# A sparse attention and a gated mixture on one core: one list of works, played in time, sets every engine's order

## The chip, the cores and the metric

The kernel runs on one core of a Trainium2 chip. The metric is the time of one execution in device microseconds. Before the change it took 1155.85 us (median of 3 runs, 1151.24 to 1165.65). A core has five engines with a queue each: TensorE (PE), VectorE (DVE), ScalarE (ACT), GpSimd (POOL) and SyncE (SP), which here only issues DMAs. Matmuls write to PSUM, which has eight banks; all the rest lives in SBUF.

## What is computed

```python
scores = scale * q @ k.T                      # 8 batches x 8 heads, 576 x 576, head size 64
scores = where(scores >= max(scores) - tau, scores, -1e9)
attn = exp(scores - max(scores)); attn /= sum(attn) + 1e-9
x = (attn @ v)  # heads side by side: batch x 576 x 512
theta = x @ w_theta
y = w_tok_r @ (x * cos(theta)) + w_tok_i @ (x * sin(theta))      # over the 576 tokens
u = x + y
out = u + maximum(u @ w_ch, 0)
```

The weights come in as 64-bit floats; the two token matrices are stacked into one, so there are three to convert.

## The kernel before

**Tiles.** Two heads make a pair; there are 32 pairs, four to a batch. A pair's scores are cut into nine *half scores* of 128 x 576 (288 in all): one for the tails of both heads (the last 64 queries, `tail_h`, `tail_l`), and eight for 128 queries of one head each. Numbers are split into a high and a low part (`qh`, `kh`, `kl`, `xh`, `xl` ...), so that products of the parts come near fp32. Keys are moved by DMA (`spread_k`) so that both parts of a query can stand on 128 partitions.

**Attention, per half score.** Four matmuls into the one pair of score banks (`s_ps`, line 293), DVE empties them with the minimum of the negated scores (`sc`, 299) and adds the threshold (312), ACT takes the exponential (316), DVE masks it and sums the row (317), PE transposes it (343, 358), ACT copies the result out of PSUM (348 to 365). After half a pair PE multiplies by the values (`o_ps`, 378).

**Mixture, per batch.** In `moe`: `angle` multiplies x by w_theta (`m_ps`, 419); ACT evicts it divided by 2 pi (`th`, 457), DVE rounds it (`km`, 462) and subtracts (463). `sines` loads a table, takes four sines, loads the table of the exponential again (476 to 485). `flip` transposes (504), `token` multiplies by the token weights (521) and adds to x (524), `split_u` splits the sum (100, 104, 109), and the last product ends in line 569 and the store, 574. The mixture of one batch runs while the attention of the next does. Its weights are read back per product from DRAM by a load on POOL's queue (193), into three buffers.

**Weights.** `load_weight` turns a 64-bit float into two fp32 terms by passes of ACT and DVE; for two matrices PE adds the two in PSUM (160, 161), for the third DVE (151). Then ACT copies the high part and DVE subtracts it for the low part (100, 109).

**Order.** PE's order is written by hand: per half score the score three half scores ahead, then some mixture work up to an even share (`fill`), then this half score's transposes. On the other engines a scheduler orders the instructions by priorities (`ATTENTION`, `SINES`) and its own estimate of time, before the kernel runs; each engine then follows its fixed order.

Of the kernel before, what the change touches and what calls it, by code (L numbers as in the profile page):

```python
# [10 lines left out]
F32 = mybir.dt.float32  # L11
# [18 lines left out]
AHEAD = 3  # L30

ATTENTION, SINES = 20, 10000

LAG = 3

ORDER = "a0 a1 s01 a2 a3f0 s23 t0f1 t1f2 t2f3 t3"
# [3 lines left out]
def tile_attn_moe(  # L40
# [10 lines left out]
):  # L51
    nc = tc.nc
    B, NP, _, D, S = qT.shape
    P = 128
# [4 lines left out]
    NK = 9  # L59

# [3 lines left out]
    ps_s = ctx.enter_context(tc.tile_pool(name="ps_s", bufs=1, space=PSUM))  # L64
    ps_t = ctx.enter_context(tc.tile_pool(name="ps_t", bufs=6, space=PSUM))

    @contextmanager
    def at(offset, step=1):

        here = tc.cur_priority  # L70
        tc.cur_priority = max(0, here + offset)
        yield
        tc.cur_priority = here + step

    ident = const.tile([P, P], F32, name="ident")
    make_identity(nc, ident)

    small = const.tile([P, 4], F32, name="small")
    tau_sb = small[:, 0 : 1]
    nc.sync.dma_start(tau_sb, tau.broadcast_to([P, 1]))  # L80

    root = math.sqrt(D)
    gate = small[:, 1 : 2]
    span = small[:, 2 : 3]
# [3 lines left out]
    half_pi = small[:, 3 : 4]  # L88
    nc.vector.memset(half_pi, 0.5 * math.pi)
# [4 lines left out]

    def pool_copy(out, in_):
        nc.gpsimd.tensor_scalar(out=out, in0=in_, scalar1=1.0, scalar2=0.0, op0=ALU.mult, op1=ALU.add)

    def copy(eng, out, in_):
        if eng is nc.scalar:
            nc.scalar.copy(out=out, in_=in_)  # L100
        elif eng is nc.gpsimd:
            pool_copy(out, in_)
        else:
            eng.tensor_copy(out=out, in_=in_)

    def split(eng_hi, eng_lo, hi, lo, src):

        copy(eng_hi, hi, src)
        eng_lo.tensor_tensor(out=lo, in0=src, in1=hi.bitcast(F32), op=ALU.subtract)  # L109

    def temp(name, dt=F32):
        return pool.tile([P, S], dt, tag="t576", name=name, bufs=4)

    def after(ins, other, wait=False):

        kind = mybir.DependencyClass.Sync if wait else mybir.DependencyClass.NoSync
        info = mybir.DependencyInfo(kind, mybir.DependencyReason.DATA)
        tc.add_manual_dep(ins.ins, other.ins.name, info, reason="order")
        return ins

    turn = [0]

    def load_weight(src, n, on_pe=True):

        w = pool.tile([P, S], F32, tag="xh", name="w", bufs=4)[:, :n]
        if src.dtype == F32:
            nc.sync.dma_start(w, src)
            yield
            return [(slice(0, n), w)]
        turn[0] += 1  # L130
        tag, bufs = ("wm", 3) if turn[0] % 2 else ("z", 3)
        raw = pool.tile([P, S, 2], U32, tag=tag, name="wraw", bufs=bufs)[:, :n]
        nc.sync.dma_start(raw, src.bitcast(U32).rearrange("p (n t) -> p n t", t=2))
        low, high = raw[:, :, 0], raw[:, :, 1]
        bits = pool.tile([P, S], U32, tag="xh", name="bits", bufs=4)[:, :n]
        mag = pool.tile([P, S], U32, tag="xl", name="mag", bufs=4)[:, :n]
        magf, bitsf = mag.bitcast(F32), bits.bitcast(F32)
        yield
        nc.scalar.activation(out=magf, in_=high.bitcast(F32), func=AF.Abs)
        nc.vector.tensor_scalar(out=magf, in0=magf, scalar1=W_LEAST, scalar2=W_MOST, op0=ALU.max, op1=ALU.min)  # L140
        yield
        nc.vector.tensor_scalar(
            out=bits, in0=mag, scalar1=3, scalar2=0x3FFFFFFF, op0=ALU.logical_shift_left, op1=ALU.bitwise_and
        )
        nc.vector.scalar_tensor_tensor(
            out=bits, in0=high, scalar=0xC0000000, in1=bits, op0=ALU.bitwise_and, op1=ALU.bitwise_or
        )
        nc.vector.tensor_scalar(out=mag, in0=bits, scalar1=0xFF800000, scalar2=None, op0=ALU.bitwise_and)
        nc.vector.scalar_tensor_tensor(out=w, in0=low, scalar=2.0**-52, in1=magf, op0=ALU.mult, op1=ALU.mult)
        if not on_pe:  # L150
            nc.vector.tensor_tensor(out=w, in0=w, in1=bitsf, op=ALU.add)
            yield
            return [(slice(0, n), w)]
        yield

        n2 = n if n <= 512 else n // 2
        got = []
        for c in range(0, n, n2):
            ps = ps_t.tile([P, 512], F32, tag="t", name="w_ps")[:, :n2]
            nc.tensor.matmul(ps, ident, bitsf[:, c : c + n2], start=True, stop=False)  # L160
            nc.tensor.matmul(ps, ident, w[:, c : c + n2], start=False, stop=True)
            got.append((slice(c, c + n2), ps))
        return got

    def load_wtok(c):
        got = yield from load_weight(w_tok[c * P : (c + 1) * P, :], S)
        for r, w in got:
            split(nc.scalar, nc.vector, wt_h[:, c, r], wt_l[:, c, r], w)

    def load_wm(which, src, c):  # L170
        got = yield from load_weight(src[c * P : (c + 1) * P, :], DM, which == 0)
        hi, lo = (pool.tile([P, DM], F32R, tag="zh4" if x == "whi" else "zl4", name=x, bufs=4) for x in ("whi", "wlo"))
        for r, w in got:
            split(nc.scalar, nc.vector, hi[:, r], lo[:, r], w)
        for i, t in enumerate((hi, lo)):
            nc.sync.dma_start(
                wm_dram[which, :, :, i, c, :].rearrange("m p e -> p m e"),
                t.bitcast(F32).rearrange("p (m e) -> p m e", e=P),
            )

    def all_loads(todo):
        for fn, a in todo:
            yield from fn(*a)

    loads = [(load_wm, (0, w_theta, c)) for c in range(NM)]
    loads += [(load_wtok, (c,)) for c in range(NK)]
    streams = [all_loads(loads[i::2]) for i in range(2)]

    late = all_loads([(load_wm, (1, w_ch, c)) for c in range(NM)])

    def get_wm(which, m):
        t = pool.tile([P, 2, NM, P], F32R, tag="wm", name=f"wm{which}", bufs=3)
        nc.gpsimd.dma_start(t, wm_dram[which, m].bitcast(F32R))  # L193
        return t

    tails = []
    for x in ("h", "l"):
        t = const.tile([P, P], F32R, name="tail_" + x)
        nc.gpsimd.memset(t.bitcast(F32), 0.0)
        tails.append(t)  # L200

    v5_t = []
    for i in range(3):
        v5 = const.tile([P, 2, D], F32, name=f"v5{i}")
        nc.gpsimd.memset(v5, 0.0)
        v5_t.append(v5)

    xT = {}
    pairs = {}

    def move(out, in_):
        nc.sync.dma_start(out.bitcast(F32), in_.bitcast(F32))  # L212

    def load_raw(n, src, name):
        raw = temp(name)
        nc.sync.dma_start(raw, src[n // NP, n % NP].rearrange("j d s -> (j d) s"))
        return raw

    def prepare_q(n):
# [492 lines left out]
```

## Time and profile before

| | |
|---|---|
| median of 3 runs | 1155.85 us |
| profiled execution | 1148.71 us |
| its span | 1146.9 us |
| busy: PE, DVE, ACT, POOL | 1033.3, 821.2, 682.8, 271.2 us |
| mean granted clock of PE | 0.987 |
| DMA: packets, data | 95116, 143.07 MB |

A matmul is pipelined: its busy time (about 0.3 us) is longer than the distance to the next (0.13 us), so a busy PE need not be at its pace. A wait is put down to what came last. Lines are those of the kernel before.

### The profile page before, as it was taken

The numbers are of one execution on the slowest core, as the hardware profiler recorded it, in microseconds if no ns is written. First come the engines' busy times: TensorE is split into PE (matmuls) and PEld (weight loads), VectorE is DVE, ScalarE is ACT, GpSimd is POOL, SyncE is SP. The second block draws the span as 40 slices with busy tenths as digits, with TensorE's granted clock in tenths as the row PEclk, the third lists the DMA queues.
The fourth block names the chain that finished last, engine by engine and source line by source line (L and its number), as shares of the span: only waits on it lengthen the run. The fifth ranks groups of instructions, "written<-read, shape, count | busy, mean of one in ns | idle before, by whom it ended". The sixth has DMA issues, their size and how long they took to land.

```text
span 1146.9 us, 21522 instructions
## 1 busy us (share of the span) xinstructions
PE 1033.3 (90%) x7608; PEld 907.0 (79%) x7608; DVE 821.2 (72%) x2105; ACT 682.8 (60%) x1324; POOL 271.2 (24%) x233
## 2 busy tenths in 40 slices
PE   2988899799989998999989998999899999899998
PEld 1666687688878877898778987898878988788898
DVE  4899776976768676776767767777767768686452
ACT  3666768655576556854567546764577555764350
POOL 0002014221143122420234213311234212430210
PEclk9989999989999999999999999999999999999999
DMA  7764544465543274444633364533544355430411
GB/s 240 205 187 116 134 119 113 125 178 143 145 119 97 68 201 118 114 103 113 177 106 96 93 180 126 133 94 90 164 118 118 96 138 159 117 86 12 140 51 60
DMA packets 95116, 143.07 MB, mean 125 GB/s; under 512 B 35488, under 2 KB 43680, under 8 KB 95008
## 3 DMA queue, kind: packets, MB, share of 16 engines
q1 hardware_dynamic: 85792, 108.12, 35.5%
q0 software_dynamic: 9216, 33.56, 10.3%
q8 instruction: 61, 1.00, 0.4%
q14 instruction: 47, 0.39, 0.1%
HBM read 71.37 MB, written 13.63 MB: 74 GB/s over the span
## 4 chain that ended last, share of the span: by engine, by line
PE 49%; DVE 15%; ACT 15%; DMA 9%; SPq 6%; issue 5%; ACTq 0%; DVEq 0%
PE y_ps L521 13%; PE s_ps L293 9%; PE o_ps L378 8%; PE m_ps L419 8%; SPq L212 6%; PE t_ps L343 5%; DVE s_sb L317 4%; DMA qraw<-in_qT_dram 3%; DVE sc L299 3%; ACT s_sb L316 3%; DMA kraw<-in_kT_dram 2%; ACT z L480 2%; DMA qq<-qraw 2%; DVE xl L109 2%; ACT L476 2%
## 5 line engine op out<-in xcount | busy, mean ns | idle before, releaser
L317 DVE SCALAR_TENSOR_TENSOR s_sb<-sc,nm,s_sb 128x576 f32<-128x576 f32 x288 | 264.2, 917 | 79.4 <-ACT s_sb L316 74.4
L316 ACT ACTIVATE s_sb<-sc,nm 128x576 f32<-128x576 f32 x288 | 224.2, 779 | 153.7 <-DVE sc L299 153.3
L299 DVE TENSOR_SCALAR_CACHE_REDUCE sc<-s_ps 128x576 f32<-128x576 f32 x288 | 216.6, 752 | 113.9 <-PE s_ps L293 111.4
L293 PE MATMUL s_ps<-k,qq 128*128 128x288 f32 x1024 | 195.1, 313 | 56.4 <-DVE sc L299 48.5
L293 PEld LDWEIGHTS s_ps<-k,qq 128*128 128x128 f32 x1024 | 151.9, 193 | 73.9 <-DVE sc L299 63.6
L348 ACT COPY a<-t_ps 128x512 f32<-128x512 f32 x256 | 147.3, 578 | 68.0 <-PE t_ps L343 67.4
L378 PE MATMUL o_ps<-a,v 128*64 128x256 f32 (+1 forms) x1280 | 175.9, 422 | 1.1 <-ACT a L350 1.0
L343 PE MATMUL t_ps<-ident,s_sb 128*128 128x128 f32 x1152 | 174.7, 275 | 0.0
L521 PE MATMUL y_ps<-wt_h,zh 128*128 128x288 f32 x576 | 165.3, 305 | 4.8 <-ACT zh L506 4.8
L521 PE MATMUL y_ps<-wt_l,zh 128*128 128x288 f32 x576 | 163.2, 301 | 0.0
L343 PEld LDWEIGHTS t_ps<-ident,s_sb 128*128 128x128 f32 x1152 | 142.6, 141 | 2.1 <-issue 0.8
L378 PEld LDWEIGHTS o_ps<-a,v 128*64 128x64 f32 x1280 | 90.4, 141 | 65.4 <-issue 12.9
L193 POOL DMA_DIRECT2D wm<-wm_dram x64 | 36.2, 565 | 349.6 <-PE m_ps L419 318.3
L521 PEld LDWEIGHTS y_ps<-wt_h,zh 128*128 128x128 f32 x576 | 108.9, 189 | 5.5 <-ACT zh L506 5.5
L521 PEld LDWEIGHTS y_ps<-wt_l,zh 128*128 128x128 f32 x576 | 109.0, 189 | 0.0
L521 PE MATMUL y_ps<-wt_h,zl 128*128 128x288 f32 x576 | 102.8, 304 | 0.0
L419 PE MATMUL m_ps<-uh,wm 128*128 128x288 f32 x512 | 84.5, 300 | 11.5 <-ACT uh L100 11.5
L228 POOL TENSOR_TENSOR qraw<-qraw,qh 128x576 fp32r<-128x576 f32 x31 | 44.3, 1429 | 212.7 <-ACT qh L226 206.8
L419 PE MATMUL m_ps<-xh,wm 128*128 128x288 f32 x512 | 90.0, 305 | 3.0 <-ACT a L348 2.5
L492 POOL TENSOR_TENSOR z<-z,xT 128x576 f32<-128x576 f32 x56 | 82.8, 1508 | 29.4 <-ACT z L480 29.4
L521 PEld LDWEIGHTS y_ps<-wt_h,zl 128*128 128x128 f32 x576 | 83.5, 189 | 0.0
L419 PEld LDWEIGHTS m_ps<-uh,wm 128*128 128x128 f32 x512 | 72.0, 188 | 13.8 <-ACT uh L100 13.3
(90 smaller groups left out, 1541.5 us busy)
## 6 DMA issues: line engine op xcount, KB each, us to landing
wm<-wm_dram POOLq DMA_DIRECT2D x64, 512.0 KB, 4.6
qraw<-in_qT_dram SPq DMA_DIRECT2D x32, 288.0 KB, 3.0
kraw<-in_kT_dram SPq DMA_DIRECT2D x32, 288.0 KB, 3.2
k<-kh SPq DMA_DIRECT2D x64, 144.0 KB, 2.5
k<-kl SPq DMA_DIRECT2D x64, 144.0 KB, 2.7
out_dram<-xT SPq DMA_DIRECT2D x32, 288.0 KB, 4.5
qq<-qh SPq DMA_DIRECT2D x64, 128.0 KB, 2.4
qq<-qraw SPq DMA_DIRECT2D x64, 128.0 KB, 2.4
```

The costliest lines, as they stand in the source:

```text
L212: nc.sync.dma_start(out.bitcast(F32), in_.bitcast(F32))
L228: eng.tensor_tensor(out=lo, in0=raw, in1=hi.bitcast(F32), op=ALU.subtract)
L293: nc.tensor.matmul(ps[:, h, :HS], st, kk[:, h * HS : (h + 1) * HS], start=(x == 0), stop=(x == len(parts) - 1))
L299: nc.vector.tensor_scalar(out=sc.rearrange("p (a b) -> p a b", a=2), in0=ps[:, :, :HS], scalar1=-1.0, scalar2=None, op0=ALU.mult, op1=ALU.min,
L316: nc.scalar.activation(out=e, in_=u.ps[j], func=AF.Exp, bias=nm[:, j : j + 1], scale=-1.0)
L317: nc.vector.scalar_tensor_tensor(out=e, in0=u.ps[j], scalar=nm[:, 2 + j : 3 + j], in1=e, op0=ALU.is_le, op1=ALU.mult, accum_out=u.pr.rows[ ...
L343: nc.tensor.transpose(out=tp[:, c * P : (c + 1) * P], in_=u.sf[:, k0 + c * P : k0 + (c + 1) * P], identity=ident)
L348: nc.scalar.copy(out=t.a[:, :, j, q0 : q0 + P], in_=tp.rearrange("p (c q) -> p c q", c=4))
L378: nc.tensor.matmul(o[64 * j : 64 * j + 64, :w], st, mv, start=(c == 0), stop=(c == 4))
L419: nc.tensor.matmul(tiles[h][:, :HS], wm[:, a, c, :], parts[c][bb][:, hs], start=(count[h] == 0), stop=(count[h] == 11))
L492: lo_eng.tensor_tensor(out=zi, in0=zi, in1=x, op=ALU.mult)
L521: nc.tensor.matmul(ps[:, :HS], z, w, start=(n == 0), stop=(n == len(work) - 1))
```

## The change

The file is written anew around a list. Each piece of work is entered with its engine, a fixed duration, the works that it needs, the buffers that it takes and a rank; `Plan.run` plays the list, always taking the work that can start first, by rank where several can, and emits the instructions in that order, for all five engines. Attention's half score h has the rank 3.2 h; its passes have offsets from it; the mixture's works are spread over the ranks of the next batch.

```diff
+    def run(self):
+            for e in engines:
+                for w in wait[e]:
+                    at = max(free[e], w.ready)
+                    for p, n in w.pots:
+                        at = max(at, p.soonest(n))
...
+                    best = (first, min((x for x in starts if x[0] <= first + 1e-6), key=lambda x: x[1].rank)[1])
...
+            free[w.eng] = at + w.busy
+            w.end = at + w.busy + w.lag + HOP
+            w.fn()
...
-        for r, w in got:
-            split(nc.scalar, nc.vector, wt_h[:, c, r], wt_l[:, c, r], w)
+                for k, x in enumerate(terms()):
+                    nc.tensor.matmul(bank.tile, turns if turn else ident, x[:, r], start=(k == 0), stop=False)
+                nc.tensor.matmul(bank.tile, minus, hi_of()[:, r], start=False, stop=True)
+            def low(r=r, bank=bank):
+                nc.scalar.copy(out=lo_of()[:, r], in_=bank.tile)
...
-                nc.scalar.activation(out=th[:, hs], in_=ps[:, :HS], func=AF.Copy, scale=1.0 / TURN)
-            km = temp("km")
-            nc.vector.tensor_scalar(out=km, in0=th, scalar1=MAGIC, scalar2=-MAGIC, op0=ALU.add, op1=ALU.add)
-            nc.vector.tensor_tensor(out=th, in0=th, in1=km, op=ALU.subtract)
+                    nc.vector.tensor_scalar(
+                        out=th.tile[:, hs], in0=bank.tile[:, :HS], scalar1=MAGIC, scalar2=-MAGIC, op0=ALU.add, op1=ALU.add
+                    )
+                def rest():
+                    less(nc.vector, th.tile[:, hs], bank.tile[:, :HS], th.tile[:, hs])
...
-        nc.gpsimd.dma_start(t, wm_dram[which, m].bitcast(F32R))
+            nc.sync.dma_start(h.tile.bitcast(F32), wm_dram[which, m])
...
-            for r in (slice(0, 64), slice(64, P)):
-                if j == 0:
-                    move(t[r], src)
+                    move(pr.kd[j].tile[dst, :, to], pr.kk.tile[src, :, fr])
...
-            split(nc.scalar if c == NM - 1 else nc.vector, nc.vector if c == NM - 1 else nc.gpsimd, hi, lo, xT[b * NP + c])
+            us[m] = halves_of(m, "u", False, m < 3 and not last, adds, here() - STEP)
```

**Low parts of weights by PE.** PE sums the two terms of a weight and, with a negated identity, the high part; what is left in PSUM is the low part, which ACT copies out. This now holds for all three matrices. **Angles as turns.** The first matrix is scaled by 1 / 2 pi while it is converted, so the product in PSUM counts turns; DVE rounds each half of it straight from PSUM and subtracts. **Moves.** The high and low parts of queries and keys lie in one tile (`qhl`, `khl`), so that tails and keys move in half as many DMAs; a pair's values come in one load. **Other.** The mixture's weights are read back on SP's queue. The last high part of u is made on DVE, not ACT, and the first channel product of a batch takes the fourth tile last. The list's durations are constants, such as 0.76, 0.13 and 0.82 us for the three DVE passes of a half score, 0.67 for DVE's subtraction of a whole tile, and 0.131 for a matmul.

The order on SP at the start, before: `qraw`, `kraw` are the first pair's loads, `wraw` weights, `qh` and `qraw` the parts of its queries; the moves of its keys (`k_0_0`) follow.

```order
L80 DMA small<-in_tau_dram 128x1
L216 DMA qraw_93<-in_qT_dram 128x576
L133 DMA wraw<-in_w_theta_dram 128x1024 x4
L133 DMA wraw<-in_w_tok_dram 128x1152
L216 DMA kraw_109<-in_kT_dram 128x576
L216 DMA qraw_209<-in_qT_dram 128x576
L212 DMA tail_h<-qh_95 64x64 x2
L212 DMA tail_l<-qraw_93 64x64 x2
L212 DMA qq_0_103<-qh_95 64x512
```

And of the change, the same place; `kd` are moved keys, `64x1152` a half with both parts.

```order
L385 DMA qraw<-in_qT_dram 128x576
L385 DMA kraw<-in_kT_dram 128x576
L466 DMA v<-in_vp_dram 128x640
L245 DMA wraw<-in_w_theta_dram 128x1024
L385 DMA qraw<-in_qT_dram 128x576
L245 DMA wraw<-in_w_theta_dram 128x1024
L466 DMA v<-in_vp_dram 128x640
L217 DMA qq<-qhl 64x512
L217 DMA kd<-khl 64x1152
L217 DMA tails<-qhl 64x2x64 x2
L217 DMA kd<-khl 64x2x512
L217 DMA qq<-qhl 64x512
```

The load of the keys moved ahead of the weights, two loads of weights moved behind the first moves, and the moves of keys stand among those of queries and tails.

The order on DVE in the middle, where a batch's x is split and its first angle is done, before (`sc` empties scores, `s_sb` masks):

```order
L109 TENSOR_TENSOR xl<-xT_4327,xh 128x576
L109 TENSOR_TENSOR xl<-xT_4730,xh 128x576
L317 SCALAR_TENSOR_TENSOR s_sb,rows_4749<-sc,nm,s_sb 128x576
L312 TENSOR_SCALAR nm<-nm,small 128x1
L299 TENSOR_SCALAR sc,nm<-s_ps 128x576
```

And of the change, the split and, a little later, an angle's halves:

```order
L214 TENSOR_TENSOR xl<-xT,xh 128x576
L511 TENSOR_SCALAR sc,nm<-s_ps 128x576
L214 TENSOR_TENSOR xl<-xT,xh 128x576
L522 TENSOR_SCALAR nm<-nm,small 128x1
L537 SCALAR_TENSOR_TENSOR s_sb,rows<-sc,nm,s_sb 128x576
L511 TENSOR_SCALAR sc,nm<-s_ps 128x576
L537 SCALAR_TENSOR_TENSOR s_sb,rows<-sc,nm,s_sb 128x576
L522 TENSOR_SCALAR nm<-nm,small 128x1
L537 SCALAR_TENSOR_TENSOR s_sb,rows<-sc,nm,s_sb 128x576
L511 TENSOR_SCALAR sc,nm<-s_ps 128x576
L817 TENSOR_SCALAR th<-m_ps 128x288
```

Between the two subtractions for x an emptying now stands, and the roundings of angles (817) read PSUM by halves between the passes of attention.

The order on SP in the middle of the change (before, the loads `wm` stood in POOL's queue):

```order
L998 DMA out_dram<-xT 128x576
L217 DMA kd<-khl 64x1152
L358 DMA wm_3357<-wm_dram 128x1024
L217 DMA kd<-khl 64x2x512
L217 DMA kd<-khl 64x1152
L385 DMA qraw<-in_qT_dram 128x576
L217 DMA kd<-khl 64x2x64
L217 DMA kd<-khl 64x2x512
```

A load of the mixture's weights, which waits for PE to free one of three buffers, moved in between two moves of a pair's keys.

## Rows read from the trace of the kernel before

**Rows 1.** timeline of TensorE: start us, busy us, engine, line, operation, count
```profile
144.55 2.38 PE L378 MATMUL o_ps<-a,v 128*64 128x256 f32 x20
...
603.71 0.60 PE L343 MATMUL t_ps<-ident,s_sb 128*128 128x128 f32 x4
604.14 0.60 PE L504 MATMUL z_ps<-ident,z 128*128 128x128 f32 x4
605.07 2.91 PE L378 MATMUL o_ps<-a,v 128*64 128x320 f32 x20
```

**Rows 2.** stretches: length, busy us (x instructions) by engine, PE clock, DMA share, GB/s
```profile
0.00:146.90 146.90, 106.37 (x603) 78.34 (x603) 115.80 (x309) 89.87 (x175) 19.46 (x25) 0.98 0.61 173
146.90:289.00 142.10, 126.02 (x931) 110.85 (x929) 109.15 (x275) 86.42 (x167) 35.00 (x28) 0.96 0.53 141
289.00:421.30 132.30, 124.03 (x943) 110.17 (x941) 95.54 (x247) 81.95 (x160) 35.45 (x29) 0.99 0.46 122
...
818.50:949.90 131.40, 124.02 (x941) 110.19 (x942) 95.49 (x247) 82.01 (x160) 35.41 (x29) 0.99 0.46 122
949.90:1075.20 125.30, 117.93 (x906) 105.47 (x906) 85.94 (x226) 74.59 (x146) 28.93 (x25) 1.00 0.35 92
1075.20:1146.90 71.70, 64.09 (x474) 62.00 (x473) 32.50 (x60) 21.62 (x37) 10.79 (x11) 1.00 0.23 75
sum 1146.90, PE 1033.30 PEld 907.05 DVE 821.19 ACT 682.85 POOL 271.20; mean PE 114.81 PEld 100.78 DVE 91.24 ACT 75.87 POOL 30.13
```

**Rows 3.** chain that ended last, in order of time: start us, us, what
```profile
1119.59 9.17 PE y_ps L521 x69
```

**Rows 4.** TensorE's waits, 289.0 to 949.9 us: total, times, longest
```profile
PE s_ps L293 <- DVE sc L299: 21.8, 24, 2.2
PE z_ps L504 <- ACT th L457: 10.2, 5, 2.0
PE m_ps L419 <- ACT uh L100: 7.6, 5, 1.5
```

**Rows 5.** timeline around the end of a block of sines, [idle before <- releaser]
```profile
581.64 1.28 ACT L485 ACT_TABLE_LOAD   x1
582.94 0.41 ACT L457 ACTIVATE th<-m_ps 128x288 f32<-128x288 f32 x1
583.49 0.91 PE L504 MATMUL z_ps<-ident,z 128*128 128x128 f32 x4 [2.04 <-ACT th L457]
```

**Rows 6.** ten microseconds around it, columns as in rows 2
```profile
580.00:590.00 10.00, 7.82 (x51) 5.60 (x51) 6.16 (x11) 7.79 (x16) 5.64 (x4) 0.83 0.30 92
```

**Rows 7.** timeline of TensorE at the start
```profile
22.71 0.58 PE L293 MATMUL s_ps<-k,qq 128*128 128x288 f32 x1 [6.23 <-DMA k<-kh]
```

**Rows 8.** instructions by form: shapes, count | busy us, mean ns | idle, releaser
```profile
L109 DVE TENSOR_TENSOR wt_l<-w_ps,wt_h 128x288 fp32r<-128x288 f32 x18 | 7.8, 449 | 0.2
L109 DVE TENSOR_TENSOR wlo<-w,whi 128x512 fp32r<-128x512 f32 x4 | 3.2, 789 | 0.7 <-ACT whi L100 0.7
L457 ACT ACTIVATE th<-m_ps 128x288 f32<-128x288 f32 x64 | 26.5, 417 | 13.0 <-PE m_ps L419 12.6
L462 DVE TENSOR_SCALAR km<-th 128x576 f32<-128x576 f32 x32 | 18.4, 573 | 28.1 <-ACT th L457 21.0 <-DMA qq<-qh 7.1
L463 DVE TENSOR_TENSOR th<-th,km 128x576 f32<-128x576 f32 x32 | 31.9, 996 | 0.3
L524 DVE TENSOR_TENSOR xT<-y_ps,xT 128x288 f32<-128x288 f32 x64 | 28.8, 450 | 9.1 <-PE y_ps L521 9.1
L109 DVE TENSOR_TENSOR ul<-xT,uh 128x576 fp32r<-128x576 f32 x8 | 6.0, 754 | 0.7 <-ACT uh L100 0.7
L109 DVE TENSOR_TENSOR xl<-xT,xh 128x576 fp32r<-128x576 f32 x16 | 23.6, 1509 | 0.5 <-ACT xh L100 0.5
```

**Rows 9.** timeline of VectorE at the halves of x
```profile
557.86 3.19 DVE L109 TENSOR_TENSOR xl<-xT,xh 128x576 fp32r<-128x576 f32 x2
```

**Rows 10.** longest wait of all engines: us in total, times, longest
```profile
POOL wm L193 <- PE m_ps L419: 318.3, 47, 18.3
```

More of the change, by code (lines that the diff above doesn't have):

```diff
@@ new lines, with __init__ @@
+class Work:
+    def __init__(self, eng, busy, fn, need, rank, lag, takes):
+        self.eng, self.busy, self.fn, self.rank, self.lag, self.takes = eng, busy, fn, rank, lag, takes
+        self.need = [w for w in need if w is not None]
+        self.frees, self.users, self.end, self.ready = [], [], None, 0.0
+        self.left = len(self.need)
+        self.pots = [(p, sum(h.pot is p for h in takes)) for p in {h.pot: 0 for h in takes}]
+        for w in self.need:
+            w.users.append(self)
@@ new lines, in tile_attn_moe, with pot, hold, get @@
+    pots = {}
+    def pot(name, n):
+        pots[name] = Pot(name, n)
+    for name, n in (
[3 rows of a table added]
+    ):
+        pot(name, n)
+    def hold(name):
+        return Hold(pots[name])
+    def get(h, shape, dt=F32, name=None, tag=None):
+        tag = tag or h.pot.name
+        p = psum if tag in ("pair", "bank") else pool
+        return p.tile(shape, dt, tag=f"{tag}{h.slot}", name=name or tag, bufs=1)
+    PACE, TURN_PACE = 0.131, 0.109
+    def on_pe(n, fn, need, rank, takes=(), pace=PACE, lag=0.165, extra=0.0):
+        return plan.add("PE", n * pace + extra, fn, need, rank, lag + 0.027, takes)
@@ L121, in tile_attn_moe @@
[L121 to L163, printed above, removed]
@@ L196, in tile_attn_moe, with less @@
[L196 to L209, printed above, removed]
+    def less(eng, out, a, b):
+        eng.tensor_tensor(out=out, in0=a, in1=b, op=ALU.subtract)
     def move(out, in_):
         nc.sync.dma_start(out.bitcast(F32), in_.bitcast(F32))
[L214 to L217, printed above, removed]
@@ new lines, in tile_attn_moe, with load_wm, load @@
+    last_wm = [None]
+    def load_wm(which, m, rank):
+        h = hold("wm")
+        def load():
+            h.tile = get(h, [P, 2, NM, P], F32R, f"wm{which}")
+            nc.sync.dma_start(h.tile.bitcast(F32), wm_dram[which, m])
+        h.load = on_sp(load, wm_ready[which] + [last_wm[0]], rank, (h,), 4.2)
+        last_wm[0] = h.load
+        return h
+    halves = [(n, i, j) for n in range(B * NP) for i in (4, 0, 1, 2, 3) for j in range(2 if i < 4 else 1)]
+    pairs = {}
+    score_pe = {}
@@ L667 @@
+    plan.run()
 def kernel(**inputs):
```

1122 lines of the change are left out of this document (699 added, 423 removed), and 3 rows, old and new, of the table pots.

## The prediction

> **What bounds the kernel now.** I cut the span where the last value product of each batch ends (144.55 + 2.38 = 146.9 us for the first [rows 1], and so on) and read the busy times of the stretches [rows 2]. Over the span TensorE (PE) is busy 1033 of 1147 us, VectorE (DVE) 821; but a busy PE is not a PE at its pace, and the stretches differ. There are four kinds: the first batch of attention with the conversion of the weights (146.9 us), the second with the rest of it (142.1), then five alike, 660.9 us from 289.0 to 949.9, 132.2 each (attention of one batch with the mixture of the batch before), a last batch of attention (125.3), and a tail of 71.7 in which only the last mixture is left.
>
> What would PE need for one of the five? Its paces stand in dense rows: 69 token products in 9.17 us, 0.133 each [rows 3]; four transposes from 603.71 to 604.14, 0.108 each; a value product of 2.91 or 2.38 us [rows 1]. One batch holds 152 score, 192 channel and 216 token matmuls (560 x 0.133 = 74.5 us), 220 transposes (23.8) and four value products of either size (21.2): 119.5 us. The period of 132.2 is 12.7 above it. PE's three largest waits over the five periods are 21.8, 10.2 and 7.6 us [rows 4], 7.9 per period; the other 4.8 are small waits, a lower clock, and pauses that hide in the modelled ends of matmuls. So the middle is bound by PE, with a tenth of it holes, and the reader should see that what PE waits for is late for reasons of order. At 583.49 it waits 2.04 us for a PSUM bank whose angles ScalarE (ACT) reads only at 582.94, behind the table load that ends a block of sines [rows 5]; in the ten microseconds around it the granted clock is 0.83, between 2.4 and 1.2 GHz [rows 6]. The scores wait for a DVE that is late with emptying their banks.
>
> The first stretch is bound elsewhere: DVE is busy 115.8 of 146.9 us, PE 106.4 [rows 2]. The first whole scores start at 22.71 us, after 6.23 us of waiting for moved keys [rows 7].
>
> **The change part by part.** *The start.* In SP's new order the first keys are loaded third, and the moves that the first whole scores need stand second to seventh behind the loads, high and low part in one transfer; before, they stood behind weights, tails, the queries' moves and a load of values. Keys can then be split near 8 us, moved by 12 and landed some 2.5 us later: scores at about 15 instead of 22.71. I take 7 us off; the bounds are 0 (weights hold DVE and ACT instead) and 8.
>
> *Low parts of the weights.* In the first stretch DVE loses 18 subtractions of 0.449 us and 4 of up to 0.789 [rows 8], 11 us. PE gains 18 products of 288 columns and 4 of 512 (0.133, and 512/288 x 0.133 = 0.236): 3.3 us, hidden, since PE idles 40 there. ACT gains 22 copies of about 0.45 us (its nearest row is the eviction of 288 columns, 0.417), 10 us on an engine busy 90 of 147 [rows 2]; covered, and worth those 10 if it weren't. DVE is the bound, so I take 10 off, and 3 more because the list spreads thirteen conversions over 36 half scores where the order before has them within 22, so that DVE runs dry less. Stretch 1: 146.9 - 7 - 10 - 3 = 127. In stretch 2 DVE loses an addition and a subtraction, 0.789 each at most, for four pieces of the third weight matrix (6 us), and PE takes on about 5; PE was busy 126.0 of the 142.1 us [rows 2]. I take off the 6, and 6 of the 16 idle for the new order: 130.
>
> *Angles.* ACT loses 64 evictions of 0.417 us (26.5 us, 3.3 per batch). DVE loses 0.573 + 0.996 per angle and gains four passes over half a tile from PSUM. No row has these; the nearest is the addition of half a tile from PSUM, 0.450 [rows 8]. From below half of the rounding from SBUF bounds a pass (0.29), from above a subtraction of a whole tile (0.754). With 0.45, 1.80 stands against 1.57, 0.9 us per batch more; DVE idles 37 us per period and hides it, or 0.9 are lost. What it buys is that no bank of angles waits for a block of sines: PE's 2.0 us per period go, and with them 1.2 of the 1.7 us (0.17 x 10) that the clock costs there.
>
> *The order.* The wait for the last high part of u (7.6 us in five periods, 1.5 each) goes, since that copy leaves ACT and the first channel product takes the fourth tile last. Of the 4.4 us per period for which scores wait for DVE I take off 2.9: emptying has a low rank number, so that it is next when its scores are done, but a pass under way is never broken off. Another 0.8 are taken for the small waits. Per period: 132.2 - 2.0 - 1.2 - 1.5 - 2.9 - 0.8 = 123.8.
>
> *Contention, which the list does not know.* Its durations are fixed. The same subtraction of a whole tile takes DVE 0.754 us for the low part of u and 1.509 for that of x [rows 8]: at 557.86 two of the latter take 3.19 us [rows 9] while GpSimd (POOL) makes its own two. In the new order of DVE these two still stand close together. By the rows 1.5 us of the score waits stay for it, as above. The Trainium skill ("SBUF — State Buffer", Who interferes with whom) says that GpSimd and a DVE pass that contend for their shared port pair do not share it, the second one is fully blocked; the trace agrees (1.509 against 0.754), and by that rule the list's 0.67 us for x is too short in every period.
>
> *The last two stretches.* In the eighth some 5 us of the same go: 120. In the tail PE has 60.0 us of work behind the last value product where it had 61.6, by the same paces, and idles 7.6 [rows 2]; I take 1.6 and 1 off: 69.
>
> Sum: 127 + 130 + 5 x 123.8 + 120 + 69 = 1065 us of span, against 1146.9. The profiled execution's own time was 1148.7, 1.8 above its span, and the median shown, 1155.85, is 1.006 of that. So (1065 + 1.8) x 1.006 = **1073 us**.
>
> **The rivals.** *Slip eats the middle.* Every engine now follows a fixed order, so a pass of 1.5 us where the list has 0.67, or a late transfer, holds all that stands behind it. For it: the rows of xl. Against it: DVE and ACT were in an order fixed beforehand, too, and one that knew less. The middle then stays at 132.2, and the last two stretches where they were: 127 + 130 + 661 + 125 + 71.7 = 1115, 1124 us in time.
>
> *PE nearly full.* Holes and clock loss gone, the period is PE's own 119.5 us: 127 + 126 + 5 x 119.5 + 116 + 67 = 1033, 1041 us. Against it: 4.8 us per period stand in no large wait.
>
> *Little moves*: the change doesn't do what it says. DVE still bounds the first two stretches, at 140 each, and the middle gains 2 us per period: 140 + 140 + 651 + 124 + 71 = 1126, 1135 us, and up to the old time.
>
> *Slower: the mixture's weights block SP.* Their 64 loads move from POOL's queue to SP's. On POOL they waited 318.3 us for PE to give up a buffer, in 47 waits of 6.8 us on average [rows 10], and nothing on the path stood behind them. On SP one now stands between two moves of a next pair's keys. If the list thinks a buffer free when it is not, the keys behind it are late, and the scores with them: 6.8 us for each of 32 pairs are 218 us, 1292 in time. It decides for slower from 3.3 us per pair on (106 us, from 1073 to 1179, 2% above the median). Against it: the list has played PE's release itself, and keys have about two half scores (132.2 / 36 = 3.7 us each) in hand.
>
> **How the numbers follow.** Forecast, periods of 121 to 127 us: 0.62, which is 1058 to 1090. PE nearly full: 0.10. Slip: 0.15. Little moves: 0.08. Slower: 0.05. The range goes from 1035, just under the second case, to 1125, which takes in the slip; the last two stay out. The forecast's own range is 1050 to 1100. Faster by over 2%, about what a measurement of this kernel can tell from no change, is below 1132.7: the first three cases and a little of the fourth, 0.88; within 2% 0.07; slower 0.05.
>
> **What would show it.** In the profile after: first whole scores near 15 us and the first batch's end near 127; periods of 122 to 126 between the same points; no wait of PE for an angle's eviction, and no ten microseconds in the middle with a clock below 0.9; scores waiting for DVE about 1.5 us per period; xl still twice as long as ul on DVE. The forecast is wrong if periods stay above 129, which a wait of SP for PE among a pair's keys, or of ACT for a late transfer, would explain, or if they fall to 120, for then the unnamed 4.8 us were waits after all.

## The result and the profile after

The changed kernel takes **1083.61 us** (median of 4 runs, 1080.86 to 1087.21) where the kernel before, measured beside it, takes 1155.66: a ratio of 0.937, with a 95% interval of 0.930 to 0.944. It is faster by 6.3%, and 10.6 us above the forecast of 1073, inside the forecast's own range of 1050 to 1100. Of one kernel below, one execution of four ran at a granted clock of 0.75 and took 1322.29 us; the figure given for it is that of the other three.

The profiled execution has a span of 1078.8 us. Cut at the same points as before, where the last value product of each batch ends, it looks like this (columns: stretch and its length, busy time and count on PE, PE's weight loads, DVE, ACT and POOL, granted clock, DMA share, GB/s). The rows that answer to them are [rows 2].

```profile
core 0: us, PE busy (x) PEld busy (x) DVE busy (x) ACT busy (x) POOL busy (x), PEclk, DMA share, GB/s
0.00:126.20 126.20, 101.37 (x629) 76.57 (x629) 103.67 (x288) 92.46 (x184) 16.40 (x18) 1.00 0.75 204
126.20:258.20 132.00, 128.96 (x954) 112.02 (x952) 103.79 (x276) 86.35 (x164) 31.74 (x21) 1.00 0.56 150
258.20:383.90 125.70, 121.42 (x943) 109.33 (x941) 94.15 (x257) 80.03 (x151) 30.91 (x21) 1.00 0.50 130
383.90:511.20 127.30, 123.38 (x943) 110.90 (x942) 93.76 (x257) 80.05 (x151) 31.12 (x21) 0.99 0.49 128
...
889.00:1011.30 122.30, 119.08 (x914) 106.77 (x912) 87.07 (x240) 73.04 (x139) 25.16 (x17) 0.99 0.37 99
1011.30:1078.80 67.50, 62.17 (x460) 60.31 (x460) 35.88 (x69) 17.82 (x28) 3.04 (x2) 1.00 0.23 75
```

The other three periods are 125.0, 127.7 and 125.1 us, so five of them take 630.8 where they took 660.9.

| stretch | before | forecast | after |
|---|---|---|---|
| first | 146.9 | 127 | 126.2 |
| second | 142.1 | 130 | 132.0 |
| five periods, each | 132.2 | 123.8 | 126.2 |
| eighth | 125.3 | 120 | 122.3 |
| tail | 71.7 | 69 | 67.5 |
| span | 1146.9 | 1065 | 1078.8 |

Of the 13.8 us that the span is above the forecast, 11.8 lie in the five periods. There the groups of PE's waits, from 258.2 to 889 us, are now two (engine, tile and line, what ended the wait: us in total, times, longest). They answer to [rows 4]:

```profile
PE s_ps L497 <- DVE sc L511: 10.9, 14, 1.6
PE m_ps L775 <- ACT a L583: 9.0, 5, 1.8
```

The two old waits by ACT, for `th` and for `uh`, are gone, and the scores wait half as long. The second line is new. The timeline shows its place (start, duration, engine, line, operation, count; in brackets the idle time before it and what ended that), once in every period at the end of a block of sines; it answers to [rows 5]:

```profile
406.91 1.28 ACT L852 ACT_TABLE_LOAD   x1
410.13 0.67 ACT L856 ACTIVATE z<-th 128x576 f32<-128x576 f32 x1
410.83 0.82 DVE L817 TENSOR_SCALAR th<-m_ps 128x288 f32<-128x288 f32 x2 [0.49 <-ACT z L856]
412.11 1.07 ACT L583 COPY a<-t_ps 128x512 f32<-128x512 f32 x2
412.75 1.33 PE L775 MATMUL m_ps<-xh,wm 128*128 128x288 f32 x4 [1.80 <-ACT a L583]
```

DVE could round the next angle only when the last sine had read the old one, at 410.80: both stand in buffers of the kind `raw`, of which there are three. Until then the angle's two halves sat in two of the six shared PSUM banks, transposes waited in others for ACT, and PE found none for its next product. The clock falls behind it in the second and the fourth period, though the wait is as long in the others (1.7 to 1.8 us in all five); here is a stretch of ten microseconds, to set beside [rows 6]:

```profile
410.00:420.00 10.00, 8.05 (x51) 6.66 (x52) 6.76 (x21) 8.25 (x16) 6.17 (x5) 0.83 0.33 82
```

At the start PE's first products come at 13.23 us and the first whole scores at 17.71, against 22.71 in [rows 7], with no wait of their own: PE was busy with a weight's low part until then.

```profile
17.07 0.80 PE L302 MATMUL w_ps<-whi,minus 128*128 128x512 f32 x1
17.71 0.70 PE L497 MATMUL s_ps<-kd,qq 128*128 128x288 f32 x4
```

### The profile page after: what moved, and what is told of

It reads as the page before. It is cut to its first block, busy times and chain, and to the rows that moved or that the text cites. A ratio compares the mean times of both kernels' runs of the same rounds, so it can differ in the third digit from the quotient of the medians.

```text
span 1078.8 us, 21076 instructions
## 1 busy us (share of the span) xinstructions
PE 1022.4 (95%) x7650; PEld 905.0 (84%) x7650; DVE 800.1 (74%) x2152; ACT 669.9 (62%) x1269; POOL 231.1 (21%) x162
## 4 chain that ended last, share of the span: by engine, by line
PE 76%; DVE 8%; ACT 7%; DMA 5%; SPq 2%; issue 2%; POOL 0%; ACTq 0%; POOLq 0%; DVEq 0%
PE y_ps L933 22%; PE o_ps L650 13%; PE s_ps L497 12%; PE m_ps L775 12%; PE t_ps L572 9%; PE z_ps L885 3%; DMA qraw<-in_qT_dram 2%; DVE sc L511 2%; PE w_ps L301 2%; DMA kd<-khl 2%; SPq L217 2%; DVE xl L214 1%; PE t_ps L607 1%; DVE s_sb L537 1%; PE rb_ps L685 1%
## 5 line engine op out<-in xcount | busy, mean ns | idle before, releaser
L537 DVE SCALAR_TENSOR_TENSOR s_sb<-sc,nm,s_sb 128x576 f32<-128x576 f32 x288 | 247.1, 863 | 97.8 <-ACT s_sb L529 95.6
L497 PE MATMUL s_ps<-kd,qq 128*128 128x288 f32 x1024 | 186.1, 303 | 22.9 <-DVE sc L511 22.3
L497 PEld LDWEIGHTS s_ps<-kd,qq 128*128 128x128 f32 x1024 | 147.7, 188 | 35.8 <-DVE sc L511 32.1
L650 PE MATMUL o_ps<-a,v 128*64 128x256 f32 (+1 forms) x1280 | 170.2, 412 | 0.0
L933 PE MATMUL y_ps<-wt_l,zh 128*128 128x288 f32 x576 | 168.0, 308 | 0.0
L214 POOL TENSOR_TENSOR qhl<-qraw,qhl 128x576 fp32r<-128x576 f32 x31 | 46.4, 1497 | 460.6 <-ACT qhl L397 380.4
L650 PEld LDWEIGHTS o_ps<-a,v 128*64 128x64 f32 x1280 | 87.8, 137 | 61.2 <-issue 10.6
L933 PE MATMUL y_ps<-wt_h,zl 128*128 128x288 f32 x576 | 114.0, 306 | 0.0
L868 POOL TENSOR_TENSOR z<-z,xT 128x576 f32<-128x576 f32 x56 | 78.2, 1432 | 83.4 <-ACT z L855 83.4
L775 PE MATMUL m_ps<-uh,wm 128*128 128x288 f32 x512 | 92.2, 302 | 0.3 <-DVE uh L211 0.3
L775 PEld LDWEIGHTS m_ps<-xh,wm 128*128 128x128 f32 x512 | 76.0, 193 | 17.1 <-ACT a L583 11.8
```

What stands on the lines that cost most here:

```text
L214: eng.tensor_tensor(out=out, in0=a, in1=b, op=ALU.subtract)
L497: nc.tensor.matmul(ps.tile[:, half, :HS], st, kk[:, half * HS : (half + 1) * HS], start=(x == 0), stop=(x == len(terms) - 1),)
L537: nc.vector.scalar_tensor_tensor(out=e, in0=sc.tile, scalar=nm.tile[:, 1:2], in1=e, op0=ALU.is_le, op1=ALU.mult, accum_out=pr.rows.tile[:, ...
L650: nc.tensor.matmul(bank.tile[64 * j : 64 * j + 64, :w], st, mv, start=(c == 0), stop=(c == 4))
L775: nc.tensor.matmul(banks[h].tile[:, :HS], wm.tile[:, a, c, :], x[:, h * HS : (h + 1) * HS], start=(key == 0), stop=(key == 11),)
L868: eng.tensor_tensor(out=zi, in0=zi, in1=xs[m].x.tile, op=ALU.mult)
```

## The experiments

Four questions were put: what the new wait costs, what the two engines' meeting on x costs, which part of the change carries the gain, and whether the list needs its durations. One thing must be known to read them: under the list an edit changes the whole order, not the edited place alone, because every work is placed anew. Differences of a few microseconds between such kernels therefore hold more than the edit, and the four executions of one kernel already spread by 2 to 12 us (6.4 in the changed one).

| kernel | us | ratio to before, 95% |
|---|---|---|
| changed | 1083.61 | 0.937 [0.930, 0.944] |
| four `raw` buffers | 1071.09 | 0.929 [0.923, 0.934] |
| x split without POOL | 1068.87 | 0.926 [0.922, 0.931] |
| both of these | 1065.18 | 0.923 [0.919, 0.928] |
| angles by ACT, under the list | 1085.13 | 0.940 [0.935, 0.945] |
| weights converted earlier | 1085.47 | 0.941 [0.937, 0.945] |
| the same, low parts by DVE | 1099.34 | 0.953 [0.948, 0.957] |
| mixture's weights on POOL's queue | 1113.10 | 0.965 [0.961, 0.969] |
| flat durations | 1177.67 | 1.022 [1.016, 1.028] |
| before, angles by DVE | 1118.06 | 0.970 [0.965, 0.975] |
| before, mixture's weights on SP | 1137.16 | 0.986 [0.981, 0.991] |
| before, both | 1117.99 | 0.970 [0.965, 0.974] |

**A fourth buffer for angles.**

```diff
-("raw", 3)
+("raw", 4)
```

> The kernel of the change with a fourth buffer for raw loads, angles and the broadcast of row sums (raw 3 to 4), nothing else edited; the list is played again with it. In the trace of the change TensorE waits 1.80 us in each period for a PSUM bank at the end of the first block of sines (412.75, 540.05). Theory A: the bank is held since VectorE cannot evict the next angle before ScalarE has read the old one in its last sine (the rounding at 410.83 waits 0.49 us for that sine), that is, for want of a buffer. Then the wait and the fall of the clock after it go, about 1.8 to 2.5 us per period, and the time falls by 10 to 17 us, to about 1070. Theory B: the bank is held by copies of transposed scores that queue behind the block on ScalarE. Then the wait stays and the time is within 4 us of the change's.

Measured: 1071.09 us, 12.5 below the changed kernel (the profiled spans differ by 10.9), as theory A has it. The line of `m_ps` is gone from PE's waits, and the one that is left is this (from the first sines of the second batch to those of the seventh):

```profile
PE s_ps L497 <- DVE sc L511: 9.8, 9, 1.6
```

Between equal points, the first table loads of successive batches, the periods fell from 125.9 to 123.8 us. In the trace DVE now rounds the next angle while the sines still run:

```profile
410.13 0.45 DVE L817 TENSOR_SCALAR th<-m_ps 128x288 f32<-128x288 f32 x1
411.06 0.67 ACT L856 ACTIVATE z<-th 128x576 f32<-128x576 f32 x1
```

So the new wait, with the clock behind it, was nearly all that the forecast of the periods had missed. The line stands in all five kernels here that have the list with measured durations, angles on DVE and three `raw` buffers (5.8 to 9.0 us in five periods), and in neither of the two with four.

**The split of x on DVE alone.** In the changed kernel the low parts of the first two tiles of x are POOL's, the others DVE's, at the same time:

```profile
385.96 3.06 POOL L214 TENSOR_TENSOR xl<-xT,xh 128x576 fp32r<-128x576 f32 x2 [7.94 <-ACT xh L209]
386.49 1.23 DVE L211 CAST xh<-xT 128x576 fp32r<-128x576 f32 x1
387.77 1.86 DVE L214 TENSOR_TENSOR xl<-xT,xh 128x576 fp32r<-128x576 f32 x1
389.56 0.75 DVE L511 TENSOR_SCALAR_CACHE_REDUCE sc<-s_ps 128x576 f32<-128x576 f32 x1
390.36 0.80 PE L497 MATMUL s_ps<-kd,qq 128*128 128x288 f32 x4 [1.59 <-DVE sc L511]
```

```diff
-            sx.append(halves_of(c, "x", c < 3, c < 2, xs[c].normal + prev.us, rank))
+            sx.append(halves_of(c, "x", c < 3, False, xs[c].normal + prev.us, rank))
```

> The kernel of the change with all four low halves of x on VectorE, none on GpSimd. Theory A (contention): in the change the copy of the high half takes 1.13 us and the low half 1.24 us on VectorE while GpSimd makes its two, and TensorE waits 1.6 us per period for the scores to be emptied behind them. With GpSimd out of the way the copy takes 0.46 and each of four low halves 0.75, the wait of scores for VectorE falls from 2.2 us per period to under 1, and the time falls by 4 to 9 us. Theory B: VectorE has 1.5 us more to do per period and is the reason itself; the wait stays or grows and the time is within 3 us of the change's or above.

Measured: 1068.87 us, 14.7 below. DVE's groups for the split of x, first of the changed kernel, then of this one (count, busy us, mean ns):

```profile
L214 DVE TENSOR_TENSOR xl<-xT,xh 128x576 fp32r<-128x576 f32 x16 | 19.6, 1237 | 0.0
L211 DVE CAST xh<-xT 128x576 fp32r<-128x576 f32 x8 | 9.0, 1131 | 0.0
```

```profile
L214 DVE TENSOR_TENSOR xl<-xT,xh 128x576 fp32r<-128x576 f32 x32 | 22.8, 752 | 1.5 <-ACT xh L209 1.5
L211 DVE CAST xh<-xT 128x576 fp32r<-128x576 f32 x8 | 3.6, 453 | 0.0
```

DVE makes twice as many low parts and copies the last high one, and spends 26.4 us on it instead of 28.6: POOL's help had cost DVE time. PE's wait for the scores over the same stretch as above shrinks from 10.9 to 3.6 us:

```profile
PE m_ps L775 <- ACT a L583: 6.2, 5, 1.8
PE s_ps L497 <- DVE sc L511: 3.6, 12, 0.7
```

The time fell further than the 4 to 9 us expected, and further than that wait. The periods give 1.8 us each, 9 in all. Another 6.3 us come before the first sines, which stand at 146.2 instead of 152.5 us, as in the new order most products with the angles' weights begin at 129 instead of 142 us; but 4.0 of them are lost again up to the sines of the second batch (133.5 us instead of 129.5). That looks like the list placing works anew. The run doesn't tell how much of it the contention had held up.

**Both edits.**

> Both edits, the fourth buffer and the low halves of x on VectorE. If both waits are separate (both theories A) the gains add up: 14 to 25 us below the change, 1060 to 1070, periods of 122 to 123 us. If TensorE's unnamed 2.7 us per period grow instead, the time stays above 1072.

Measured: 1065.18 us, 18.4 below the changed kernel, where the two alone gave 12.5 and 14.7. It is the fastest kernel of the study. Its PE waits from 258.2 to 889 us:

```profile
PE s_ps L497 <- DMA wm<-wm_dram: 3.9, 1, 3.9
PE s_ps L497 <- DVE sc L511: 3.0, 4, 1.5
```

The first line is a single wait at the start of the middle that neither edit had alone, and its period is 129.5 us long; the others lie between 121.4 and 124.3. With it the five average 124.0, no better than the buffer alone. So part of what the sum lacks went into a new wait on a transfer. Which one is open: the line names what landed last, but scores read moved keys and queries, not `wm`.

**The angles, from both sides.** Under the list ACT evicts them again, and DVE rounds a whole tile:

```diff
-                k = on_dve(0.37, whole, [w] + zs.get((m, "t"), []), rank - 2 * STEP, (th,) if h == 0 else ())
-                r = on_dve(0.37, rest, [k], rank - 2 * STEP)
+                e = on_act(0.31, out_, [w] + ready_w, rank - 2 * STEP, (th,) if h == 0 else ())
...
+                k = on_dve(0.37, whole, list(ready_w), rank - 2 * STEP, (km,))
+                r = on_dve(0.67, rest, [k], rank - 2 * STEP)
```

> The kernel of the change with one part undone: ScalarE copies the angles out of PSUM (64 copies of about 0.42 us), VectorE rounds and subtracts them from SBUF, with a buffer of their own for the rounded part; the list is played with these works. Theory A, as in the prediction: an eviction of angles on ScalarE comes to stand behind a block of sines and holds a PSUM bank, so TensorE waits some 2 us more per period: 12 to 20 us above the change, 1095 to 1103. Theory B: the list finds another place for the evictions; within 5 us of the change, and the gain of the middle is the order's.

Measured: 1085.13 us, 1.5 above the changed kernel and not to be told from it: the time of theory B, but not its reason. The evictions did come to stand behind the block of sines, in every period, and PE waits there as the prediction said:

```profile
414.63 1.28 ACT L867 ACT_TABLE_LOAD   x1
416.40 0.41 ACT L817 COPY th<-m_ps 128x288 f32<-128x288 f32 x1
416.56 0.80 PE L775 MATMUL m_ps<-xh,wm 128*128 128x288 f32 x4 [1.41 <-ACT a L583]
```

These waits come to 6.9 us in five periods, where the changed kernel has 9.0 at the same place for want of a buffer; the scores wait 13.2 instead of 10.9. So two kernels are compared that lose about alike behind the block, for different reasons. The changed kernel with a fourth buffer is 14.0 us faster than this one, about what theory A expected of the eviction; this one with a fourth buffer wasn't tried.

And in the kernel before, without a list, DVE rounds them from PSUM:

```diff
-                nc.scalar.activation(out=th[:, hs], in_=ps[:, :HS], func=AF.Copy, scale=1.0 / TURN)
+                nc.vector.tensor_scalar(
+                    out=th[:, hs], in0=ps[:, :HS], scalar1=MAGIC, scalar2=-MAGIC, op0=ALU.add, op1=ALU.add
+                )
+                nc.vector.tensor_tensor(out=th[:, hs], in0=ps[:, :HS], in1=th[:, hs], op=ALU.subtract)
```

> The kernel before with one part of the change: the first weight matrix is scaled by 1 / 2 pi while PE sums it, and VectorE rounds and subtracts the angles straight from PSUM by halves; no list. Theory A, the step of the prediction: no bank of angles waits for ScalarE's block of sines, so TensorE's wait of 2.0 us per period for a transposed z goes and with it the fall of the clock, 2 to 3.2 us per period: 14 to 22 us below the kernel before, 1132 to 1142. Theory B (after the run in which ScalarE evicts angles under the list and nothing is lost): the wait was one of order, and here another eviction behind the sines takes its place; within 6 us of the kernel before.

Measured: 1116.91 us, a larger gain than the 14 to 22 us of theory A. The same kernel was run again for its trace:

> The kernel before with one part of the change: the angles' whole turns are rounded by DVE straight from PSUM, half a tile at a time, and ScalarE evicts no angle; no list. Timed earlier at 33 us under the kernel before; this run is for its trace. Theory A (each batch gives back the same): the middle periods fall from 132.2 to 127.5-128.5 us, TensorE's wait for m_ps on ACT's th is gone (10.2 us over five batches before), and the 10 us around the end of the sines no longer fall to a clock of 0.83. Theory B (the gain lies at the start and the end): the middle periods stay above 130.5 us, and the first stretch and the tail lose 15 us or more.

Measured: 1118.06 us, 35.7 below the kernel before. The first sines stand where they stood (170.1 against 169.9 us), from there to the sines of the second batch it is 8.8 us shorter, and each period 3.7 (132.2 to 128.5). PE's longest waits over five periods now, beside [rows 4]:

```profile
PE s_ps L296 <- DVE sc L302: 11.7, 14, 1.3
PE o_ps L381 <- DVE zl L509: 7.9, 5, 1.6
PE m_ps L422 <- ACT uh L102: 7.6, 5, 1.5
PE m_ps L422 <- DVE th L462: 3.8, 5, 0.8
```

The wait for ACT's `th` is gone, the scores' wait is halved, two smaller ones came. No ten microseconds of the five periods have a clock below 0.97 any more. So this part does alone, per period, about what was foretold of it (3.2). Under the list the same loss is there with ACT's evictions, and with DVE's the missing buffer put another of like size in its place.

**The mixture's weights on SP's queue, from both sides.**

```diff
-            nc.sync.dma_start(h.tile.bitcast(F32), wm_dram[which, m])
+            nc.gpsimd.dma_start(h.tile.bitcast(F32), wm_dram[which, m])
```

> The kernel of the change with the 64 loads of the mixture's weights on GpSimd's queue again (ranked and played in the list there), nothing else. Theory A (the queue does not matter, since the list places the loads where buffers are free): within 5 us of the change. Theory B, the prediction's slower rival in small: on SP these loads hold back key moves, so without them the time is 5 to 15 us below the change. Theory C: issuing on GpSimd meets VectorE's passes and GpSimd's own, and the time is 5 us or more above.

Measured: 1113.10 us, 29.5 above the changed kernel, the largest price of the three parts that were undone. That is theory C by size. The first sines come 8.1 us later, the periods are 130.2 instead of 125.9 us. POOL waits 201.7 us for PE, from 258 to 889 us, before it may issue loads. PE's waits in the five periods, from 291.8 to 943.0 us:

```profile
PE s_ps L497 <- DVE sc L511: 14.8, 21, 2.1
PE m_ps L775 <- ACT a L583: 8.8, 5, 1.8
PE m_ps L775 <- DVE xh L211: 3.2, 5, 0.7
```

Against the two lines of the changed kernel PE's waits grew by 1.4 us per period, of the 4.3 that a period is longer. Much of the rest is a lower clock: ten stretches of ten microseconds lie below 0.97 here, two in the changed kernel. In some periods it falls in two places, one of them behind a wait for the scores:

```profile
521.33 0.79 PE L497 MATMUL s_ps<-kd,qq 128*128 128x288 f32 x4 [2.07 <-DVE sc L511]
```

```profile
520.00:530.00 10.00, 8.67 (x57) 7.55 (x58) 7.49 (x23) 5.10 (x12) 1.93 (x2) 0.83 0.48 134
530.00:540.00 10.00, 8.30 (x52) 7.83 (x52) 9.29 (x20) 5.82 (x11) 3.33 (x3) 0.83 0.33 108
```

What makes DVE late there is a transfer: its masking pass waited 5.10 us for ACT's exponential of 518.45, and ACT, in its fixed order, had stood still for the next pair's queries.

```profile
516.58 0.78 ACT L393 ACTIVATE qraw<-qraw,small 128x576 f32<-128x576 f32 x1 [4.35 <-DMA qraw<-in_qT_dram]
519.26 0.96 DVE L537 SCALAR_TENSOR_TENSOR s_sb<-sc,nm,s_sb 128x576 f32<-128x576 f32 x1 [5.10 <-ACT s_sb L529]
```

That load was issued at 508.89 and landed after 7.6 us, where the median here is 4.4. Besides, DVE's copy `xh` next to POOL's two passes takes 2.17 us on average here, 1.13 in the changed kernel. Why loads on POOL's queue bring both about was not followed; that it is the low halves behind POOL's waits is argued only. In the kernel before the same move, the other way:

> The kernel before with one other part alone: the mixture weights are loaded on SP's queue instead of POOL's; no list. Under the list the move the other way cost 29.5 us. Theory A (POOL's low halves stand behind the weights' waits, whatever sets the order): faster by 10 to 30 us, 1123-1143 us. Theory B (in an order that the code's generators make, the waits block SP instead, and with it the loads of the next pairs): slower, 1170 us or more, with new waits of TensorE for kd or qq behind DMA. Theory C (only where they stand matters little in this order): within 8 us of before.

Measured: 1137.16 us, 16.6 below the kernel before, in the range of theory A. The periods fall from 132.2 to 130.0 us, and PE's wait for the scores over five of them from 21.8 to 10.9. And with the angles by DVE as well:

> The kernel before with the angles rounded by DVE from PSUM and the mixture weights on SP's queue, both; no list, the low parts of the weights still subtracted on DVE. Theory A (the list is what turns both into time): the two together give at most what the angles give alone, 1110-1125 us, and the list and the low parts are worth 27 us or more. Theory B (the list adds little beside these two parts): 1085-1100 us, so that 1083.6 is reached but for the low parts' 10 to 14 us. If the load on SP blocks SP: above 1125 us.

Measured: 1117.99 us, the same as the angles alone. The scores' wait for DVE falls from 11.7 to 7.6 us over five periods, and this line of waits for moved keys rises from 1.8:

```profile
PE s_ps L296 <- DMA k<-kl: 5.9, 6, 1.4
```

The 4.1 us that one wait lost the other gained. It looks like the forecast's slower rival on a small scale, weights' loads on SP in front of a pair's keys; that these loads are what made the keys late was not followed. In the changed kernel no such line is left. What the rest of the change adds to the two edits (the list, the low parts, the halved moves and the small edits) is 1118.0 - 1083.6 = 34.4 us; no run has the list without the others.

**The low parts of the weights.** The conversions of both kernels of this pair begin at an earlier rank, and one is the other's control.

```diff
-    rank = 4.0
+    rank = -10.0
```

> Control for the next run: the kernel of the change with the conversion of weights ranked 14 us earlier (its first rank -10 instead of 4). The first stretch is bound by VectorE, which has the same work in another order, so both theories expect the change's time within 5 us.

Measured: 1085.47 us, within the spread of the changed kernel, although the first sines come 5.5 us later (158.0 against 152.5). A place at the start, then, says little about the time. And with it:

```diff
-                nc.tensor.matmul(bank.tile, minus, hi_of()[:, r], start=False, stop=True)
...
-                nc.scalar.copy(out=lo_of()[:, r], in_=bank.tile)
+                less(nc.vector, lo_of()[:, r], bank.tile, hi_of()[:, r].bitcast(F32))
```

> The control with one part undone: VectorE subtracts the high part of a weight from PSUM for the low part, as in the kernel before, for all three matrices (26 subtractions of 0.45 to 0.69 us), TensorE's products with the negated identity and ScalarE's copies go. Theory A, as in the prediction: VectorE bounds the first stretch, so it is longer by the 22 subtractions in it, 8 to 11 us, and the time 8 to 13 us above the control. Theory B: VectorE is not busy enough for that (in the change 103.7 of 126.2 us), and half or more is hidden: at most 5 us above the control.

Measured: 1099.34 us, 13.9 above its control, a little over theory A's 8 to 13. The work that went back to DVE is this, 13.7 us:

```profile
L214 DVE TENSOR_TENSOR wt_l<-w_ps,wt_h 128x288 fp32r<-128x288 f32 x18 | 8.2, 457 | 9.4 <-PE w_ps L301 8.0 <-ACT a L616 0.9
L214 DVE TENSOR_TENSOR wlo<-w_ps,whi 128x512 fp32r<-128x512 f32 x8 | 5.5, 687 | 4.1 <-PE w_ps L301 4.1
```

The size agrees with the whole, not with the places: the first sines are 3.6 us later than the control's (161.6 against 158.0), the second stretch 3.6 longer, and each period 1.0, although no weight is converted in them. The last of these looks like the list's new order again.

**Durations.** Every work of DVE and ACT is entered at 0.5 us.

```diff
     def on_dve(busy, fn, need, rank, takes=()):
+        busy = 0.5
...
     def on_act(busy, fn, need, rank, takes=()):
+        busy = 0.5
```

> The changed kernel, with every work of DVE and ScalarE entered in the list at 0.5 us instead of its measured duration (0.04 to 1.3 us); TensorE's and the transfers' durations as they are. Theory A (the order is right because the durations are): the played times of ScalarE and DVE drift, works are issued out of their order of need, and the time rises by 20 us or more, to 1104 us at least. Theory B (works that stand in the order of their due times and needs come out nearly alike, as TensorE sets the pace): within 10 us of 1083.6. Between 1094 and 1104 us neither is shown.

Measured: 1177.67 us, 94.1 above the changed kernel and slower than the kernel before. The expectation named too small a largest duration: a block of sines with its table loads is entered as one work, and in the trace it lasts from 406.91 to 412.10, 5.2 us. The load as a whole is not wrong in this kernel (DVE's some 1500 works make 750 us at 0.5 each, and 800 by the busy time of the changed kernel's page). What is wrong is single works, and none by more than that one. Its ACT and PE in one period:

```profile
450.51 1.28 ACT L854 ACT_TABLE_LOAD   x1
454.42 1.28 ACT L859 ACT_TABLE_LOAD   x1
459.74 0.33 PE L609 MATMUL t_ps<-ident,s_sb 128*128 128x128 f32 x1 [2.02 <-DVE th L216]
476.61 1.28 ACT L859 ACT_TABLE_LOAD   x1
482.69 1.33 PE L499 MATMUL s_ps<-kd,qq 128*128 128x288 f32 x4 [1.88 <-DVE sc L513]
```

```profile
460.00:470.00 10.00, 10.00 (x70) 8.05 (x69) 7.05 (x20) 4.13 (x10) 0.08 (x1) 0.83 0.21 66
480.00:490.00 10.00, 8.12 (x39) 4.92 (x38) 5.78 (x15) 3.80 (x8) 0.97 (x1) 0.66 0.48 125
```

PE's waits and the falls of the clock follow the two blocks of sines. The periods are 136.9 us instead of 125.9, and the first sines come at 182.7 instead of 152.5. Whether the block of sines alone makes most of the loss wasn't tried.

## Why the prediction was right, and where it was not

**The first two stretches**: right in sum (126.2 + 132.0 against 127 + 130), not in their terms. The 5.0 us by which whole scores start earlier answer to the 7. The low parts were put at 10 us in the first stretch; undone against their control they moved the first sines by 3.6. The forecast took DVE's busy time as the bound of that stretch, so that 11 us of work off DVE were 10 off the time. No run bears these 10 out: an earlier rank, with the same work for DVE, moved the same sines by 5.5. The kernel before with both other parts has its first sines at 169.4 us, the changed one at 152.5. Of those 16.9 us the low parts answer for some 3.6; the rest belongs to the list's order, the earlier loads and the halved moves, which no run parts from each other. That the term "3 because the list spreads the conversions" was too small is argued only.

**Angles.** "What it buys is that no bank of angles waits for a block of sines" is the step that failed. The eviction left ACT, yet its target was still read by the sines, so two banks stayed full all the same, for 1.8 us per period and a fall of the clock in two of the five. The fourth buffer took 12.5 us off, and the periods then are the forecast's 123.8. With it the sign "no ten microseconds in the middle with a clock below 0.9" holds; in the changed kernel it failed twice. The other half of the step, that evictions by ACT do wait for the block, was right: they do under the list too. The buffers' list had been there to read: three of a kind for queries, keys, angles and sums. That two passes over half a tile cost 0.45 us each was right:

```profile
L817 DVE TENSOR_SCALAR th<-m_ps 128x288 f32<-128x288 f32 x64 | 28.6, 452 | 16.5 <-PE m_ps L775 11.9 <-PE rb_ps L685 2.5 <-ACT z L856 1.0
```

**The order.** The wait for `uh` went, as said. The scores wait for DVE 10.9 / 5 = 2.2 us per period where 1.5 was taken.

**Contention** was a right cause. POOL off the split of x brought that wait to 0.7 us per period. In the timeline above DVE's copy of 386.49 lasts 1.23 us instead of 0.45, and the subtraction of 387.77 ends at 389.63, 0.61 us behind POOL's second pass (389.02), so it stood still through most of that. The Trainium skill ("SBUF — State Buffer", Who interferes with whom) says that the second of the two fully blocks until the first is done; the trace agrees nearly, for a pass of 0.75 us that began only at 389.02 would have ended 0.14 us later. "xl still twice as long as ul" was too high: 1.24 against 0.76 us, since one of the two meets POOL and the other doesn't.

**The last two stretches** were 2.3 over and 1.5 under.

**The rivals.** The slip came about in a milder form, if at all: the periods gave back 2.4 us each, not 8.4. Of PE's 20 us of waits in five periods, those for the scores stand, where they were looked at, beside passes that the list has too short; the others come from a shortage of buffers that the list knows. PE nearly full did not: even the best kernel's undisturbed periods are 121.4 to 124.3 us, above the 119.5 of PE's own paces. That loads on SP would block it was rightly held unlikely. The reason given, that the list plays PE's release, fits: without a list and with the angles on DVE, waits for keys grew by 4.1 us in five periods, in the changed kernel there are none. What the forecast left out altogether is that this move is a gain, of 16.6 us alone in the old order and 29.5 under the list, for a reason that is only in part known.

**The sum** was within 1%, and that is in part luck, as errors of both signs met: the move of loads gave a gain that was not written down, the low parts less in the first stretch than was, and a buffer took back 12.5 us.

## What to carry to other kernels

When an eviction moves to another engine, look at who still reads the buffer that it writes to: the bank comes free only when the target does, and one more buffer was worth 12.5 us here. When an edit seems to be worth nothing, look in both traces for what its place holds now: the angles' 35.7 us were 1.5 under the list, where a wait for a buffer had taken the place of the one that went. Parts don't add up by themselves: 35.7 and 16.6 us were 35.8 together. A list played in time needs its durations, for flat ones cost 94 us, more than the change had gained; and help from an engine that shares a port with DVE can cost more than it brings.

## What the runs showed of the hardware

A copy of one tile on DVE, `xh`, was slowed by POOL no less than the subtraction of two: 0.453 us without POOL and 1.131 beside it, against 0.752 and 1.237. A wait of PE of about 1.8 us is followed by ten microseconds at a clock of 0.83, between 1.2 and 2.4 GHz, in some periods and not in others with the same wait (those of 127.3 and 127.7 us against those of 125.0 to 125.7). And DVE's masking pass, one shape throughout, takes 0.917 us in the kernel before, 0.863 in the changed one, 0.901 in the fastest and 1.000 in the kernel before with the angles on DVE; what slows it wasn't tried.
